# Moving GpSimd's arithmetic to VectorE and storing T by head in a chunked delta-rule attention with two expert layers

## Chip, cores and metric

One core of one Trainium2 chip runs the whole program. The metric is device time in microseconds (us) of one execution; lower is better. The kernel before takes 1076.54 us, the median of 3 runs (1076.4 to 1076.81).

## What is computed

Three layers follow each other. The first is the one that the change touches: for each of 4 batches and 8 heads a 48 x 48 state is carried over 768 tokens, and every token's key corrects it.

```python
state = zeros((B, H, D, D))                      # B, H, D = 4, 8, 48
for t in range(S):                               # S = 768, k_n = normalised k
    y[:, :, t] = einsum('bhd,bhde->bhe', q[:, :, t], state)
    v_old = einsum('bhde,bhd->bhe', state, kt)
    state = state + bt * einsum('bhd,bhe->bhde', kt, vt - v_old)
```

The 3072 result rows of 384 numbers then go through a top-1 layer of 8 experts (384 to 1024 to 384, with a gate) and a gated dense layer (384 to 1536 to 384).

## The kernel before

The sequence is cut into 24 chunks of 32 tokens (`CH`, `NSTEP`). One chunk is a **step** s; four steps are a **group** g, two steps a pair u. The four batches lie in the 128 partitions, 32 tokens each. Inside a chunk the recurrence is solved with a triangular matrix T of 32 x 32 for each head and batch, so that a step is a few matmuls, written out in order in the loop of `Attention.run` (line 751):

- **KS** (line 778): state times key, 16 matmuls with stationary operand `KB[...][:, p, :, h]`; VectorE makes `W` from it (line 780).
- **Y**, first half (line 795): state times query from `QB`, 16 matmuls.
- **U** (line 804): T times W, 16 matmuls. The stationary operand is taken out of `TBD` with a step of 32 elements between its 64 columns (line 805). ScalarE writes the fp16 high part `UH[:, 0]` (line 807), VectorE the low part (line 811).
- **XTP** (`gate_t`), the expert gate's transposes for the step before; **GP** (`gp_mm`), the key products of step s + 11, 12 of its 16 matmuls here and 4 at the end of the step; there is GP only for s below 13.
- **Sps** (line 844): the state's update from `KBD` and `UH`, in three passes of which only the third reads the low part; ScalarE copies the state to `SH`.
- **Y**, second half (line 850), from `PBD` and `UH`; **GL** (`gate_l`), six gate matmuls whose stationary operand `xt[:, c, r]` has its 64 columns side by side.

Each fp32 matmul stands in the trace as two records, so the blocks KS, Y and U have 32 each, GP 24 and 8, GL 12.

Every engine runs its instructions in the order of the program. What is put between the instructions above comes from hand-set places and from a planner, `Filler` (line 99): it holds the chain that makes the next group's T and the gate's small operations, with a planned duration for each, and `fil.run(budget)` issues as many as the budget covers. A step has a budget of `TA` = 2.4 us between the W and the low part of UH (line 806) and of `TB` = 4.2 us (`TC` = 3.8 us from step 12 on) at its end (line 906). At the end of a group, lines 910 to 912 issue whatever is left of the next group's T at one go.

The T of a group is made by `prep` (line 330: transposing, normalising, `scale`) and `inv_ops` (line 387: 31 columns j, each one product `tmp<-X,Lt` and one sum `X<-X,tmp` over min(j + 1, share) rows of 31 - j elements, in one or two parts). Rows from `SHE[g]` on (24 for group 2, 20 for groups 3 to 5; none for group 1) are GpSimd's. `last` (line 441) turns X into `XT`; `expand_t` (line 379) copies the 8 columns that the first step of the group needs into `TBD`, and later, in that step, the other 24: two quarters by VectorE (line 813), two by ScalarE (line 874).

GpSimd's other work in the steps: `scale` for groups 2 to 5 (line 341, all 32 rows), `v_mul` (202), `p_split` (276), `p_split_lo` (290), `kh_split_lo` (316), and `scatter` (574) with its indirect DMA. SyncE (SP) issues all other DMAs, among them `kexp` (322) and `expand` (293), each four DMAs that spread `KH` and `PHL` into `KBD` and `PBD`.

Of the kernel before, what the change touches and what calls it, by code (L numbers as in the profile page):

```python
# [7 lines left out]
F32 = mybir.dt.float32  # L8
# [5 lines left out]
ALU = mybir.AluOpType  # L14
# [20 lines left out]
LA = 11  # L35
# [9 lines left out]
XE = (0, 1, 2, 3, 4, 5)  # L45
# [4 lines left out]
WE = 1.0  # L50
TC = 3.8
NR = 8
Q2 = 0.0
GS = 6
KA = 1
SHE = (0, 32, 24, 20, 20, 20)
TA = 2.4
TB = 4.2
W0 = 36
# [39 lines left out]
class Filler:  # L99
# [41 lines left out]
class Attention:  # L141
# [5 lines left out]
    def run(self, small, acc, zero_fill, small_loads):  # L147
# [23 lines left out]
        QB = [cp.tile([128, 2, 64, 8], F32, name=f"QB{i}") for i in range(2)]  # L171
        TBD = [(cp if i else ep).tile([128, 2, 1024], F32, name=f"TBD{i}") for i in range(2)]
        PBD = [cp.tile([128, 2, 16, 4, 32], F16, name=f"PBD{i}") for i in range(2)]
# [18 lines left out]
        def load_kth(u):  # L192
            t = wk.tile([128, 2, 48, 8], F32, tag="kth", name="kth", bufs=1)
            SP.dma_start(out=t.rearrange("p s d h -> p s (d h)"), in_=a["ktok"][:, 2 * u : 2 * u + 2])
            KTOK[u] = t
# [5 lines left out]

        def v_mul(s):
            g, s4 = divmod(s, 4)
            v = VT[s // 2][:, s % 2].rearrange("p (h e) -> p h e", h=8)
            G.tensor_tensor(out=v, in0=v, in1=nt[:, g, 8 * s4 : 8 * s4 + 8].unsqueeze(2).to_broadcast([128, 8, 48]), op=ALU.mult)

# [68 lines left out]

        def p_split(u):
            g, i = divmod(u, 2)
            if g:
                pm = GPM[g][1][:, 16 * i : 16 * i + 16]
                G.tensor_tensor(out=pm, in0=pm, in1=rnt[:, g, 16 * i : 16 * i + 16].unsqueeze(2).to_broadcast([128, 16, 32]), op=ALU.mult)  # L280
            else:
                pm = PM.pop(u)
            G.tensor_tensor(out=pm, in0=pm, in1=mask.unsqueeze(1).to_broadcast([128, 16, 32]), op=ALU.mult)
            PHL[u] = wk.tile([128, 2, 16, 32], F16, tag="PHL", name="PHL", bufs=4)
            PMS[u] = pm
# [3 lines left out]

        def p_split_lo(u):  # L290
            G.tensor_tensor(out=PHL[u][:, 1], in0=PMS.pop(u), in1=PHL[u][:, 0], op=ALU.subtract)

# [23 lines left out]
        def kh_split_lo(u):  # L316
            KH, src = KHG[u], KTOK.pop(u)
            for s in range(2):
                G.tensor_tensor(out=KH[:, s, 1], in0=by_head(src[:, s]), in1=KH[:, s, 0], op=ALU.subtract)

# [9 lines left out]
        def prep(g):  # L330
# [9 lines left out]

            def scale(E, j0, j1, i0):
                L = Lt[:, j0:j1, i0:]
                E.tensor_tensor(out=L, in0=L, in1=x[:, j0:j1].unsqueeze(2).to_broadcast([128, j1 - j0, 32 - i0]), op=ALU.mult)
                E.tensor_tensor(out=L, in0=L, in1=nbr[:, g, i0:].unsqueeze(1).to_broadcast([128, j1 - j0, 32 - i0]), op=ALU.mult)


# [18 lines left out]
            ]  # L365
            sc = [(0.0, 0.0, lambda: scale(G, R, 32, R))]
            if R:
                sc.append((R / 12.0, 0.0, lambda: scale(V, 0, R, 0)))
            return ops, sc

        XTS, others = {}, []

        def share_rows(n):
# [5 lines left out]
        def expand_t(g, bs, ks):  # L379
            for E, b in zip((V, V, A, A), range(4)):  # L380
                if b in bs:
                    r = slice(32 * b, 32 * b + 32)
                    src = XTS[g][r].rearrange("p i b -> p (i b)").rearrange("p (i b) -> p i b", b=32)
                    dst = TBD[g % 2][r, b % 2].rearrange("p (i b) -> p i b", b=32)
                    (E.copy if E is A else E.tensor_copy)(out=dst[:, :, ks], in_=src[:, :, ks])

        def inv_ops(g, share=32):
# [53 lines left out]
            def last(F):  # L441
                share_rows(99)
                XT = wk.tile([128, 32, 32], F32, tag="XT", name="XT", bufs=1)
                V.transpose(out=XT.rearrange("p i b -> p (i b)"), in_=X.rearrange("p k i -> p i k"))
                F.t += 1.135
                F.ready = F.t
                F.done = g
                XTS[g] = XT
                if g == 0:
                    V.memset(zl, 0.0)  # L450
                if g in XE:
                    expand_t(g, range(4), slice(0, 8))
                else:
                    for b in range(4):
                        r = slice(32 * b, 32 * b + 32)
                        SP.dma_start(out=TBD[g % 2][r, b % 2], in_=XT[r].rearrange("p i b -> p (i b)"))

# [169 lines left out]
        SP.dma_start(out=be, in_=a["beta"])  # L627
        SHz = wk.tile([128, 2, 384], F32, tag="SH", name="SH", bufs=2)
        V.memset(SHz.rearrange("p b c -> p (b c)"), 0.0)
# [67 lines left out]
        p_split(0)  # L697
        zero_fill(SP, 0, TBD[1])
        p_evac(2)
# [5 lines left out]
        gp(9)  # L705
        zero_fill(SP, 1, TBD[1])
        load_kth(1)
# [27 lines left out]
        load_kth(2)  # L735
        zero_fill(SP, 2, TBD[1])
        busy(Sps[0], D.get(0, 0))
# [13 lines left out]
        for s in range(NSTEP):  # L751
# [12 lines left out]
            beside(s, "load", engines)  # L764
            if s2 == 0 and 0 < s < NSTEP - 2:
                kh_split_lo(u + 1)
            if s2 == 1 and u + 3 < NSTEP // 2:
                p_split(u + 3)
            if s > 0:
# [16 lines left out]
            if s2 == 0 and 0 < s < NSTEP - 2:  # L786
                expand(PBD[(u + 1) % 2], PHL.pop(u + 1))
                if half:
                    load_kth(u + 2)
                kexp(u + 1)  # L790

# [46 lines left out]
            if not last:  # L838
                SH = wk.tile([128, 2, 384], F32, tag="SH", name="SH", bufs=2)
# [676 lines left out]
```

## Time and profile before

| What | us |
|---|---|
| median of 3 runs | 1076.54 |
| the profiled execution | 1079.49 |
| its span, first to last instruction | 1077.8 |
| TensorE (PE) busy in it | 1022.6 |
| VectorE (DVE) busy | 569.2 |
| GpSimd (POOL) busy | 430.2 |
| ScalarE (ACT) busy | 416.9 |

The 24 steps lie between 65 and 348 us of the span; what is before prepares group 0, what is behind is the two expert layers, and the change leaves both as they are but for T's layout. Busy shares are averages; a wait counts only where it ends last. PEclk is the granted share of TensorE's 2.4 GHz: 1.00 is 2.4 GHz, 0.50 is 1.2 GHz, and a mean between them says how the stretch is divided between the two levels. Matmuls are pipelined: a record's duration says little, and the time from the start of one block to the start of the next is what the block costs.

### The profile page before, as it was taken

Reading aid. Unit: us, or ns where it says so; the run is one execution under the profiler, and the core shown is the slowest. Engines: PE = TensorE matmul, PEld = TensorE weight load, DVE = VectorE, ACT = ScalarE, POOL = GpSimd, SP = SyncE. Lnnn points to the kernel's source line nnn. Section 1 sums busy time; section 2 is a strip of 40 time slices with the busy share of each in tenths; the row PEclk is TensorE's granted clock in tenths of the full one; section 3 lists DMA queues with packets and bytes.
Section 4 is the critical chain, followed back from the end, with each engine's and each line's share of the span. In section 5 each row is a group of like instructions: output and inputs, shape, how many; then the busy total and the mean of one; then the engine's idle time right before and its main releaser. Section 6 shows DMA issues by size and latency. Waiting matters only on the chain. (4 is left out here: it accounts for less than half of the span.)

```text
span 1077.8 us, 22538 instructions
## 1 busy us (share of the span) xinstructions
PE 1022.6 (95%) x9111; PEld 926.5 (86%) x9112; DVE 569.2 (53%) x1376; ACT 416.9 (39%) x892; POOL 430.2 (40%) x460
## 2 busy tenths in 40 slices
PE   8788999997899999899899899999999999999997
PEld 8777989897898988789889888888888888888886
DVE  6978899989965587667673364511211211211211
ACT  6644646474563444454445232311212222212111
POOL 8455456665733235444444134322322311321322
PEclk8976865566569999999999999999999999999999
DMA  7899977644485365455643222000000000000000
GB/s 187 200 175 201 193 151 142 141 92 86 88 160 133 126 208 155 150 160 171 181 117 117 46 60 74 23 23 1 18 12 1 30 1 1 30 1 1 30 1 30
DMA packets 162622, 100.11 MB, mean 93 GB/s; under 512 B 108025, under 2 KB 152002, under 8 KB 162514
## 3 DMA queue, kind: packets, MB, share of 16 engines
q1 hardware_dynamic: 159442, 89.17, 35.8%
q0 software_dynamic: 3072, 9.46, 2.4%
q8 instruction: 73, 1.20, 0.5%
q14 instruction: 35, 0.29, 0.1%
HBM read 74.94 MB, written 15.80 MB: 84 GB/s over the span
## 5 line engine op out<-in xcount | busy, mean ns | idle before, releaser
L1437 DVE TENSOR_TENSOR gf<-gf,g 128x512 f32<-128x512 f32 x72 | 49.5, 688 | 312.0 <-PE g L1429 310.3
L938 POOL TENSOR_TENSOR gsl<-gf,gsh 128x512 fp32r<-128x512 f32 x68 | 88.7, 1305 | 272.1 <-ACT gsh L937 272.1
L1436 ACT ACTIVATE gf<-g 128x512 f32<-128x512 f32 x72 | 43.0, 597 | 190.8 <-PE g L1429 188.8
L937 ACT CAST gsh<-gf 128x512 fp32r<-128x512 f32 x69 | 42.8, 620 | 144.4 <-DVE gf L1437 142.5
L87 DVE TENSOR_TENSOR X<-X,tmp 128x60 f32<-128x60 f32 (+25 forms) x282 | 96.1, 367 | 1.2
L87 DVE TENSOR_TENSOR tmp<-X,Lt 128x60 f32<-128x60 f32 (+25 forms) x282 | 94.7, 362 | 1.9
L1403 PE MATMUL o<-woh,gsl 128*128 128x384 f32 x272 | 87.3, 339 | 0.0
L1403 PE MATMUL o<-wol,gsh 128*128 128x384 f32 x272 | 86.5, 337 | 0.0
L1118 DVE SCALAR_TENSOR_TENSOR hl<-h,hh 128x460 fp32r<-128x460 f32 (+7 forms) x57 | 33.1, 580 | 61.6 <-ACT hh L1117 61.4
L1429 PE MATMUL g<-yl,wgh 128*128 128x512 f32 x216 | 62.6, 395 | 0.0
L1429 PE MATMUL g<-yl,wvh 128*128 128x512 f32 x216 | 62.3, 395 | 0.0
L1077 PE MATMUL y<-hh,w2h 128*128 128x460 f32 (+6 forms) x168 | 60.8, 362 | 1.2 <-ACT hh L1117 1.0
L1403 PE MATMUL o<-woh,gsh 128*128 128x384 f32 x272 | 61.7, 337 | 0.0
L1429 PE MATMUL g<-yh,wgh 128*128 128x512 f32 x180 | 61.0, 395 | 0.0
L1077 PE MATMUL y<-hh,w2l 128*128 128x460 f32 (+6 forms) x168 | 58.6, 349 | 0.0
L87 ACT ACTIVATE kth<-kth,rnt 128x48 f32<-128x48 f32 x192 | 54.8, 375 | 6.9 <-DMA kth<-in_ktok_dram 6.6
L87 PE MATMUL GP<-KT,KB 112*64 112x64 f32 x640 | 47.8, 315 | 10.2 <-POOL KH L87 7.0
L87 PE MATMUL U<-W,TBD 64*64 64x48 f32 x768 | 47.9, 292 | 8.5 <-DVE W L87 8.5
L87 PEld LDWEIGHTS GP<-KT,KB 112*64 112x64 f32 x640 | 42.6, 221 | 14.7 <-POOL KH L87 7.1
L1403 PEld LDWEIGHTS o<-woh,gsh 128*128 128x128 f32 x272 | 49.7, 188 | 5.8
L87 PEld LDWEIGHTS U<-W,TBD 64*64 64x64 f32 x768 | 44.4, 200 | 10.6 <-DVE W L87 9.2
L1055 POOL TENSOR_TENSOR w1l<-w1r,w1h 128x768 fp32r<-128x768 f32 x19 | 37.2, 1957 | 39.9 <-ACT w1h L1050 39.6
(330 smaller groups left out, 2490.4 us busy)
## 6 DMA issues: line engine op xcount, KB each, us to landing
w1r<-in_w_dram SPq DMA_DIRECT2D x32, 384.0 KB
w2r<-in_w_dram SPq DMA_DIRECT2D x32, 384.0 KB
KT<-in_st_dram SPq DMA_DIRECT2D x20, 448.0 KB
disp<-TBD SPq DMA_DIRECT2D x8, 772.0 KB
kth<-in_ktok_dram SPq DMA_DIRECT2D x12, 384.0 KB
VT<-in_vtok_dram SPq DMA_DIRECT2D x12, 384.0 KB
KBD<-KH SPq DMA_DIRECT2D x48, 96.0 KB
XG<-in_m2g_dram SPq DMA_DIRECT2D x12, 384.0 KB
```

What stands on the lines that cost most here:

```text
L87: r = f(*args, **kw)
L937: (act or nc.scalar).copy(out=hi, in_=src)
L938: eng.tensor_tensor(out=lo, in0=src, in1=hi, op=ALU.subtract)
L1055: engine.tensor_tensor(out=l, in0=self.raw[b][i], in1=h, op=ALU.subtract)
L1077: self.T.matmul(out=ys[c][:, 0:n], lhsT=w2[l][:, f % 2, 128 * c : 128 * c + 128], rhs=(hh, hl)[r], start=(f == 0 and i == 0), stop=(f == 7 ...
L1118: self.V.scalar_tensor_tensor(out=hl, in0=hp[:, 0:n], scalar=0.0, in1=hh, op0=ALU.max, op1=ALU.subtract)
L1403: T.matmul(out=ops_[m][:, 0:384], lhsT=gh[l][:, 128 * m : 128 * m + 128], rhs=wo[r][:, f], start=(f == 0 and i == 0), stop=(f == 11 and i ...
L1429: T.matmul(out=ps, lhsT=gv[w][l][:, c, 128 * f : 128 * f + 128], rhs=Y[r][c], start=(i == 0 and c == 0), stop=(i == 2 and c == 2))
L1436: A.activation(out=gf, in_=gps[0], func=AF.Sigmoid)
L1437: V.tensor_tensor(out=gf, in0=gf, in1=gps[1], op=ALU.mult)
```

## The change

`TBD` holds T as [k, b, i], k being the head and step, so that the 64 columns (b, i) of one head lie side by side. The last 24 of its 32 k are now spread by four DMAs on SP's queue (`expand_rest`) instead of by VectorE and ScalarE. In the steps, `v_mul`, `p_split`, `p_split_lo`, `kh_split_lo`, and `scale` for groups 2 to 5 run on VectorE; `scale` then skips most of the half that is zero (six instructions over 256, 192 and 256 elements). No row of the inverse is left to GpSimd. Step 0 keeps `p_split(2)`, `v_mul(2)` and the first `p_split_lo` on GpSimd. `kh_split_lo` and `p_split` move from the head of the step to behind the low part of UH, `kexp` from behind W to the step's end. `kth` gets a second buffer and `SH` loses its own. The planner's budgets change, and `spend` takes the moved work off them.

```diff
-TC = 3.8
+TC = 4.4
-SHE = (0, 32, 24, 20, 20, 20)
+SHE = (0, 32, 32, 32, 32, 32)
-TB = 4.2
+TP = 2.5
+TB = 5.8
...
+    def spend(self, dur):
+        self.t = max(self.t, self.until) + dur
...
-        TBD = [(cp if i else ep).tile([128, 2, 1024], F32, name=f"TBD{i}") for i in range(2)]
+        TBD = [(cp if i else ep).tile([128, 32, 2, 32], F32, name=f"TBD{i}") for i in range(2)]
...
-        def v_mul(s):
+        def v_mul(s, E=G):
             g, s4 = divmod(s, 4)
+            norms(g)
...
-            sc = [(0.0, 0.0, lambda: scale(G, R, 32, R))]
             if R:
-                sc.append((R / 12.0, 0.0, lambda: scale(V, 0, R, 0)))
-            return ops, sc
+                sc = [(0.0, 0.0, lambda: scale(G, R, 32, R)), (R / 12.0, 0.0, lambda: scale(V, 0, R, 0))]
+            else:
+                sc = [(0.1 + (j1 - j0) * (32 - i0) / 1200.0, GAP, lambda f=f, r=(j0, j1, i0): f(V, *r))
+                      for f in (by_row, by_col) for j0, j1, i0 in ((0, 8, 0), (8, 16, 8), (16, 32, 16))]
+            return ops + [(0.0, 0.0, lambda: normed.add(g))], sc
...
+        def expand_rest(g):
+            for b in range(4):
+                r = slice(32 * b, 32 * b + 32)
+                SP.dma_start(out=TBD[g % 2][r, 8:32, b % 2], in_=XTS[g][r, 8:32])
...
-                V.transpose(out=XT.rearrange("p i b -> p (i b)"), in_=X.rearrange("p k i -> p i k"))
+                V.transpose(out=XT.rearrange("p b i -> p i b"), in_=X.rearrange("p k i -> p i k"))
...
-                mm(out=Up[r, h], lhsT=TBD[g % 2][r].rearrange("p b k -> p (b k)")[:, 8 * s4 + h :: 32], rhs=W[r, h], start=True, stop=True)
+                mm(out=Up[r, h], lhsT=TBD[g % 2][r, 8 * s4 + h].rearrange("p b i -> p (b i)"), rhs=W[r, h], start=True, stop=True)
...
             V.tensor_tensor(out=UH[:, 1], in0=Up, in1=UH[:, 0], op=ALU.subtract)
             if s4 == 0 and g in XE:
-                expand_t(g, (0, 1), slice(8, 32))
+                expand_rest(g)
+            if s2 == 0:
+                if 0 < s < NSTEP - 2:
+                    kh_split_lo(u + 1, V)
+                    fil.spend(0.95)
+            elif u + 3 < NSTEP // 2:
+                p_split(u + 3, V)
+                fil.spend(1.2)
...
             if s + 2 < NSTEP and s:
-                v_mul(s + 2)
+                v_mul(s + 2, V)
+                fil.spend(0.48)
...
             if s2 == 1 and u + 3 < NSTEP // 2:
                 p_split_hi(u + 3)
-                p_split_lo(u + 3)
+                fil.run(TP)
+                p_split_lo(u + 3, V)
+                fil.spend(0.6)
...
+            if s2 == 0 and 0 < s < NSTEP - 2:
+                kexp(u + 1)
             beside(s, "end", engines)
-            fil.run(((TB if s + 1 + LA < NSTEP else TC) - (0.94 if s4 == 0 and g in XE else 0.0)) if s else TB0)
+            fil.run(((TB - (TP if s2 == 1 and u + 3 < NSTEP // 2 else 0.0) if s + 1 + LA < NSTEP else TC)) if s else TB0)
```

## Rows read from the trace of the kernel before

**Rows 1.** Stretches: us, then busy us of each engine, PEclk, DMA share, GB/s.

```profile
65.00:348.00 283.00, 260.76 (x4729) 245.10 (x4728) 239.38 (x727) 153.01 (x379) 149.96 (x201) 0.67 0.72 142
165.47:178.02 12.55, 12.55 (x220) 11.79 (x219) 12.08 (x43) 8.30 (x20) 8.01 (x13) 0.50 0.96 156
218.38:229.36 10.98, 10.98 (x219) 10.45 (x218) 9.31 (x34) 7.91 (x20) 6.77 (x10) 0.78 0.47 83
315.30:346.00 30.70, 29.66 (x599) 27.72 (x597) 15.01 (x46) 15.36 (x33) 12.66 (x16) 1.00 0.65 140
320.08:329.02 8.94, 8.94 (x194) 8.47 (x190) 4.50 (x12) 5.86 (x12) 4.35 (x5) 1.00 0.79 162
```

**Rows 2.** Waits between 65 and 345 us: us in total, times, longest us.

```profile
POOL PHL L87 <- ACT PHL L87: 63.2, 11, 15.7
...
PE Sps L87 <- DVE UH L87: 12.9, 6, 5.3
...
PE U L87 <- DVE W L87: 8.5, 5, 2.7
```

**Rows 3.** DVE's groups of instructions, 65 to 345 us: busy us, mean ns, idle before.

```profile
L87 DVE TENSOR_TENSOR X<-X,tmp 128x90 f32<-128x90 f32 (+34 forms) x226 | 81.5, 385 | 1.0
L87 DVE TENSOR_TENSOR tmp<-X,Lt 128x90 f32<-128x90 f32 (+34 forms) x226 | 81.0, 384 | 1.6
...
L87 DVE STREAM_TRANSPOSE XT<-X 128x1024 f32<-128x1024 f32 x5 | 9.8, 1969 | 0.3
...
L87 DVE COPY TBD<-XT 32x768 f32<-32x768 f32 x12 | 8.1, 671 | 0.1
```

**Rows 4.** DVE's timeline, 198 to 221 us: start us, duration us, instruction.

```profile
198.25 0.34 DVE L87 TENSOR_TENSOR X<-X,tmp 128x240 f32<-128x240 f32 x1
198.51 1.89 DVE L87 SCALAR_TENSOR_TENSOR nbr<-bx,be 128x32 f32<-128x32 f32 x1
...
200.92 2.32 DVE L87 TENSOR_TENSOR X<-X,tmp 128x220 f32<-128x220 f32 x1
...
212.40 0.22 DVE L87 TENSOR_TENSOR tmp<-X,Lt 128x60 f32<-128x60 f32 x1
...
220.66 0.55 DVE L87 SCALAR_TENSOR_TENSOR W<-VT,KS 128x384 f32<-128x384 f32 x1
```

**Rows 5.** POOL's timeline at the same time.

```profile
198.41 1.95 POOL L87 TENSOR_TENSOR Lt<-Lt,bx 128x1024 f32<-128x1024 f32 x1 [0.17 <-DVE bx L87]
200.55 2.44 POOL L87 TENSOR_TENSOR Lt<-Lt,nbr 128x1024 f32<-128x1024 f32 x1 [0.19 <-DVE g_pos L87]
```

**Rows 6.** PE's timeline, blocks of step 9 (1.2 GHz) and step 12 (2.4 GHz).

```profile
181.97 2.02 PE L87 MATMUL U<-W,TBD 64*64 64x48 f32 x32
183.92 0.90 PE L87 MATMUL XTP<-cst,XG 128*128 128x128 f32 x3
...
189.41 0.83 PE L87 MATMUL GL<-wgo,xt 128*64 128x16 f32 x12
190.17 0.21 PE L87 MATMUL GL<-g_oh,lt 128*128 128x32 f16 x1
...
222.36 1.98 PE L87 MATMUL U<-W,TBD 64*64 64x48 f32 x32
224.26 0.55 PE L87 MATMUL XTP<-cst,XG 128*128 128x128 f32 x3
...
228.45 0.53 PE L87 MATMUL GL<-wgo,xt 128*64 128x16 f32 x12
228.82 0.73 PE L87 MATMUL GP<-KT,KB 112*64 112x64 f32 x8
```

**Rows 7.** SP's timeline in step 0: DMAs issued.

```profile
68.50 3.38 SPq L87 DMA_DIRECT2D KB<-in_st_dram  x2
71.98 5.34 SPq L87 DMA_DIRECT2D PBD<-PHL  x4
```

More of the change, by code (lines that the diff above doesn't have):

```diff
@@ L192, in load_kth @@
         def load_kth(u):
-            t = wk.tile([128, 2, 48, 8], F32, tag="kth", name="kth", bufs=1)
+            t = wk.tile([128, 2, 48, 8], F32, tag="kth", name="kth", bufs=2)
             SP.dma_start(out=t.rearrange("p s d h -> p s (d h)"), in_=a["ktok"][:, 2 * u : 2 * u + 2])
@@ L200, in load_v @@
             VT[u] = t
-        def v_mul(s):
+        def v_mul(s, E=G):
             g, s4 = divmod(s, 4)
+            norms(g)
             v = VT[s // 2][:, s % 2].rearrange("p (h e) -> p h e", h=8)
-            G.tensor_tensor(out=v, in0=v, in1=nt[:, g, 8 * s4 : 8 * s4 + 8].unsqueeze(2).to_broadcast([128, 8, 48]), op=ALU.mult)
+            E.tensor_tensor(out=v, in0=v, in1=nt[:, g, 8 * s4 : 8 * s4 + 8].unsqueeze(2).to_broadcast([128, 8, 48]), op=ALU.mult)
         GPS = {}
@@ L274, in run, with p_split @@
         PMS = {}
-        def p_split(u):
+        def p_split(u, E=G):
             g, i = divmod(u, 2)
             if g:
+                norms(g)
                 pm = GPM[g][1][:, 16 * i : 16 * i + 16]
-                G.tensor_tensor(out=pm, in0=pm, in1=rnt[:, g, 16 * i : 16 * i + 16].unsqueeze(2).to_broadcast([128, 16, 32]), op=ALU.mult)
+                E.tensor_tensor(out=pm, in0=pm, in1=rnt[:, g, 16 * i : 16 * i + 16].unsqueeze(2).to_broadcast([128, 16, 32]), op=ALU.mult)
             else:
                 pm = PM.pop(u)
-            G.tensor_tensor(out=pm, in0=pm, in1=mask.unsqueeze(1).to_broadcast([128, 16, 32]), op=ALU.mult)
+            E.tensor_tensor(out=pm, in0=pm, in1=mask.unsqueeze(1).to_broadcast([128, 16, 32]), op=ALU.mult)
             PHL[u] = wk.tile([128, 2, 16, 32], F16, tag="PHL", name="PHL", bufs=4)
@@ L288, in p_split_hi, with p_split_lo @@
             A.copy(out=PHL[u][:, 0], in_=PMS[u])
-        def p_split_lo(u):
-            G.tensor_tensor(out=PHL[u][:, 1], in0=PMS.pop(u), in1=PHL[u][:, 0], op=ALU.subtract)
+        def p_split_lo(u, E=G):
+            E.tensor_tensor(out=PHL[u][:, 1], in0=PMS.pop(u), in1=PHL[u][:, 0], op=ALU.subtract)
         def expand(dst, src):
@@ L298, in kh_mul @@
         def kh_mul(u, half=None):
+            norms(u // 2)
             r = rnt[:, u // 2].rearrange("p (s h) -> p s h", s=4)
@@ L314, in kh_split_hi, with kh_split_lo @@
             KHG[u] = KH
-        def kh_split_lo(u):
+        def kh_split_lo(u, E=G):
             KH, src = KHG[u], KTOK.pop(u)
             for s in range(2):
-                G.tensor_tensor(out=KH[:, s, 1], in0=by_head(src[:, s]), in1=KH[:, s, 0], op=ALU.subtract)
+                E.tensor_tensor(out=KH[:, s, 1], in0=by_head(src[:, s]), in1=KH[:, s, 0], op=ALU.subtract)
         def kexp(u):
@@ L339, in prep, with by_row, by_col, scale @@
             tr = lambda o, i, d: (d, 0.0, lambda: V.transpose(out=o, in_=i))
-            def scale(E, j0, j1, i0):
+            def by_row(E, j0, j1, i0):
                 L = Lt[:, j0:j1, i0:]
                 E.tensor_tensor(out=L, in0=L, in1=x[:, j0:j1].unsqueeze(2).to_broadcast([128, j1 - j0, 32 - i0]), op=ALU.mult)
+            def by_col(E, j0, j1, i0):
+                L = Lt[:, j0:j1, i0:]
                 E.tensor_tensor(out=L, in0=L, in1=nbr[:, g, i0:].unsqueeze(1).to_broadcast([128, j1 - j0, 32 - i0]), op=ALU.mult)
+            def scale(E, *r):
+                by_row(E, *r)
+                by_col(E, *r)
             ops = [
@@ L365, in prep, with norms @@
             ]
-            sc = [(0.0, 0.0, lambda: scale(G, R, 32, R))]
             if R:
-                sc.append((R / 12.0, 0.0, lambda: scale(V, 0, R, 0)))
-            return ops, sc
+                sc = [(0.0, 0.0, lambda: scale(G, R, 32, R)), (R / 12.0, 0.0, lambda: scale(V, 0, R, 0))]
[3 more added lines that the diff above has]
+            return ops + [(0.0, 0.0, lambda: normed.add(g))], sc
+        normed = set()
+        def norms(g):
+            while g not in normed:
+                fil.step()
         XTS, others = {}, []
+        zeros = TBD[1].rearrange("p k b i -> p (k b i)").rearrange("p (b x) -> p b x", b=2)
         def share_rows(n):
@@ L382, in expand_t @@
                     r = slice(32 * b, 32 * b + 32)
-                    src = XTS[g][r].rearrange("p i b -> p (i b)").rearrange("p (i b) -> p i b", b=32)
-                    dst = TBD[g % 2][r, b % 2].rearrange("p (i b) -> p i b", b=32)
-                    (E.copy if E is A else E.tensor_copy)(out=dst[:, :, ks], in_=src[:, :, ks])
+                    (E.copy if E is A else E.tensor_copy)(out=TBD[g % 2][r, ks, b % 2], in_=XTS[g][r, ks])
+        def expand_rest(g):
+            for b in range(4):
+                r = slice(32 * b, 32 * b + 32)
+                SP.dma_start(out=TBD[g % 2][r, 8:32, b % 2], in_=XTS[g][r, 8:32])
         def inv_ops(g, share=32):
@@ L455, in last @@
                         r = slice(32 * b, 32 * b + 32)
-                        SP.dma_start(out=TBD[g % 2][r, b % 2], in_=XT[r].rearrange("p i b -> p (i b)"))
+                        SP.dma_start(out=TBD[g % 2][r, :, b % 2], in_=XT[r])
             other = [(lambda j=j: add(G, j, share, j + 1, mul(G, j, share, j + 1))) for j in range(share, 31)]
@@ L627, in run @@
         SP.dma_start(out=be, in_=a["beta"])
-        SHz = wk.tile([128, 2, 384], F32, tag="SH", name="SH", bufs=2)
+        SHz = wk.tile([128, 2, 384], F32, tag="SH", name="SH", bufs=1)
         V.memset(SHz.rearrange("p b c -> p (b c)"), 0.0)
@@ L697, in run @@
         p_split(0)
-        zero_fill(SP, 0, TBD[1])
+        zero_fill(SP, 0, zeros)
         p_evac(2)
@@ L705, in run @@
         gp(9)
-        zero_fill(SP, 1, TBD[1])
+        zero_fill(SP, 1, zeros)
         load_kth(1)
@@ L735, in run @@
         load_kth(2)
-        zero_fill(SP, 2, TBD[1])
+        zero_fill(SP, 2, zeros)
         busy(Sps[0], D.get(0, 0))
@@ L764, in run @@
             beside(s, "load", engines)
[L765 to L768, printed above, removed]
             if s > 0:
@@ L789, in run @@
                     load_kth(u + 2)
-                kexp(u + 1)
             Yp = pp.tile([128, 8, 48], F32, tag="Y", name="Y")
@@ L838, in run @@
             if not last:
-                SH = wk.tile([128, 2, 384], F32, tag="SH", name="SH", bufs=2)
+                SH = wk.tile([128, 2, 384], F32, tag="SH", name="SH", bufs=1)
                 for p, i in ((0, 0), (0, 1), (0, 2), (1, 0), (1, 1), (1, 2)) if s < LS or not SP2 else ((0, 0), (0, 1), (1, 0), (1, 1), (0, 2), (1, 2)):
@@ L872, in run @@
                     v1 = fil.add(gate_v1(g - 1), WG)
-            if s4 == 0 and g in XE:
-                expand_t(g, (2, 3), slice(8, 32))
             if s2 == 1 and u + 3 < NSTEP // 2:
                 p_split_hi(u + 3)
-                p_split_lo(u + 3)
+                fil.run(TP)
+                p_split_lo(u + 3, V)
+                fil.spend(0.6)
             if more and s:
@@ L892, in run @@
             if s < 5:
-                zero_fill(SP, s + 3, TBD[1])
+                zero_fill(SP, s + 3, zeros)
             if s == 0:
```

## The prediction

> **What bounds the kernel now.** I read the stretches first. The steps take 283 of 1078 us, and only they are touched. In them PE is busy for 260.8 us, DVE for 239.4, POOL for 150.0, and the granted clock is 0.67 [rows 1]; as the levels are 0.5 and 1.0, 34% of the stage runs at 2.4 GHz. Step 8, in which PE never pauses, takes 12.55 us at 1.2 GHz; step 12, whose blocks behind U came after the clock had risen, takes 10.98 [rows 1]. So where nothing is late the step is PE's, and the low clock costs it 1.57 us. A step without GP at 2.4 GHz takes 8.94 us, and there the clock stayed up for 30.7 us on end [rows 1].
>
> The waits come second: PE stood 12.9 us for the low part of UH and 8.5 us for W, both DVE's: 21.4 us of stage that is neither PE's work nor its clock [rows 2].
>
> Why is DVE late? Its 452 products and sums of the inverse take 162.5 us [rows 3]. The same kind of instruction takes 0.22 us for 60 elements and 0.34 for 240, but one of 220 took 2.32, and a `nbr` of 32 elements 1.89 [rows 4]. These two lie on POOL's two passes of `scale`: `nbr` starts 0.10 us behind the first and ends with it, the 2.32 ends a quarter of a microsecond behind the second [rows 4, 5]. DVE stands while POOL reads.
>
> PE's blocks come last. U's 32 records take 1.95 us at 1.2 GHz and 1.90 at 2.4: 61 and 59 ns each. GL's, also with 64 fp32 columns, take 0.76 us for 12 at 1.2 GHz and 0.37 at 2.4: 63 and 31 ns [rows 6]. U's columns lie 128 bytes apart, GL's side by side; U gets nothing from the faster clock.
>
> **DVE's account.** Slope from 60 elements (0.22) to 240 (0.34) is 0.7 ns, but W's 384 at 0.55 and 60 at 0.22 give 1.0 ns; I take 1.0 and a base of 0.16 us, 0.08 of which overlaps the next instruction (the 0.34 is followed after 0.26) [rows 4]. Added, in occupied time:
> - `v_mul`, 21 of 384 elements at 0.47: 9.9 us.
> - `kh_split_lo`, 10 pairs of 384: 9.4 us. Its source is strided; the only long strided reads on DVE are the transposes of XT, 1.97 us for 1024 [rows 3], by which 384 take 0.74, so 5.4 us more is the upper end. I take the lower, from W, the nearest in kind.
> - `p_split`, 9 pairs of 512 at 0.59, and 9 `p_split_lo`: 16 us.
> - `scale`, four groups of six instructions, 1408 elements: 4 x (1.41 + 0.48) = 7.6 us.
> - GpSimd's rows of the inverse: 84 elements in group 2 and 286 in each of groups 3 to 5, twice over: 1.9 us.
>
> That is 45 us. The twelve `TBD` copies go, at about 0.5 each (8.1 us with what they lost to POOL [rows 3]): 6 us. Net +39. Against it the inverse: five times 5456 elements less GpSimd's 942, for product and sum, are 52.7 thousand elements, 53 us, and 452 x 0.08 = 36 us of base: 89 us where the trace has 162.5 [rows 3]. So 73 us were stood out, and 239.4 becomes about 239 - 73 + 39 = 205 us. XT's transpose now also writes with a stride; its read has one already, so I take 1.97 again, at most twice that, 10 us over five.
>
> **The terms, on the profiled 1079.49 us.**
> 1. PE's waits, 21.4 us. What stays late is the end of a group. The inverse of a group needs by the planner's own durations about 26 us (18 for the columns, 4.7 for `prep` with `scale`, 1.1 for XT, 2 for the gate). From step 12 on four steps give 4 x (2.4 + 4.4) less 7.4 of `spend`, 19.8 us. Some is worked ahead in steps 4 to 11 (32.8 - 7.4 = 25.4 a group, after a start with a lead of some 4); I expect 4 us flushed at step 15 and 2 at step 19, with W queued behind on DVE and PE waiting for W. 21.4 - 6: **-15.4**; bounds 0 and -21.4.
> 2. U. At 2.4 GHz a block goes from 1.90 us to 32 x 31 ns = 0.99: -0.91. At 1.2 GHz, 61 against 63 ns: nothing. With 60% of 24 steps at 2.4 GHz: 24 x 0.6 x 0.91 = **-13.1**; bounds 0 (layout without effect) and -21.8 (all steps at 2.4 GHz).
> 3. The clock. Nothing in the trace shows the clock of such a kernel; the nearest rows are the step without GP and without waits, which kept it, and the steps with GP, which did not though PE never paused [rows 1]. Eleven steps have no GP; I give them 0.9 and the thirteen others the old 0.34: 0.60. 24 x 0.26 x 1.57 = **-9.8**; bounds +12.8 (the share falls to nothing) and -24.9 (it is 1).
> 4. T by DMA. Four DMAs of 768 pieces each join SP's queue in the first step of each group. `PBD`'s four of 1024 pieces took 5.34 us to issue [rows 7]; three quarters are 4.0. SP has a whole step to issue and land them and U of the next step waits for them. In step 0 they queue behind `KB`, until 71.9 us, so the last is issued near 76 [rows 7], while U of step 1 could start, W no longer late, at about 76: I take **+1.5** once, between 0 and 4. They delay what is behind them on SP, `PBD` and the next loads, each needed a step later.
>
> Edits that I cost at nothing: ScalarE loses its copies and is busy for 153 of 283 us [rows 1]; `kexp` goes later, past `expand_rest` and `load_v` on SP, and may wait there for `kh_split_lo`, but `KBD` is needed in the middle of the next-but-one half step, some 10 us on (if that cover went, Sps would wait for 5 us of issue); one `SH` is enough, since KS and Y have read it, in PE's order, before Sps ends; `kth`'s second buffer only loosens.
>
> Sum: -15.4 - 13.1 - 9.8 + 1.5 = -36.8, so 1042.7 for the profiled execution; the median is 3.0 below that execution, so **1040** for the runs.
>
> **A rule that says otherwise.** At 2.4 GHz the 64 columns of GL cost 31 ns and those of U 59 [rows 6]. The Trainium skill, "TensorE: Matmul & The Clock Gate", section "LDWEIGHTS (loading the stationary operand)", says that the load takes the number of columns over 1.2 GHz and names nothing else; for 64 that is an estimate of 53 ns whatever the layout, and term 2 would be nothing. The trace disagrees at 2.4 GHz, where GL is below it, and agrees at 1.2.
>
> **The rivals.**
> - **Layout without effect.** U stays at 59 ns because its 64 x 64 tiles or its 48 moving columns set the pace, not the gaps (GL has 128 rows and 16 moving columns). Term 2 falls: 1053. For it: U differs from GL in all of these. Against: at 1.2 GHz the two cost the same [rows 6], so rows and moving columns don't part them there; the layout is left as the reason that only GL gains from the clock. 8%.
> - **The clock doesn't follow.** Steps 8 to 12 sat at 1.2 GHz with PE unbroken, so waits alone don't hold it down. Share 0.34: terms 2 and 3 are -7.4 and 0: 1079.5 - 15.4 - 7.4 + 1.5 - 3 = 1055. 20%.
> - **DVE becomes the bound.** 205 us in the 20 steps before the last inverse is done are over 10 us each, as much as a step with GP at 2.4 GHz and more than one without. If the bursts keep PE's waits at half, the strided split costs its 5 us and the clock follows the waits: 1079.5 - 8 - 7.4 + 1.5 - 3 = 1063. 12%.
> - **Slower: DVE takes over POOL's wait.** `p_split_lo` needs ScalarE's cast of `PHL`, which needs Y of the same step. POOL stood for that cast for 63.2 us in 11 waits, 5.7 us each [rows 2], with nothing urgent behind it. On DVE the filler and W stand behind it. PE has 1.3 us of cover (Y's 1.9 us less W's 0.55), so nine odd steps lose 9 x (5.7 - 1.3) = 40 us against the 36.8 gained: 1080. It decides from 36.8 / 9 + 1.3 = 5.4 us of standing. Against: `p_split`, `v_mul` and `fil.run(TP)`, 2.5 us by the plan, go first, and POOL's waits count from when it ran out of work. 8%.
>
> **How the numbers follow.** The forecast, all four terms in their middle, has 52%; it spans 1022 (all waits gone and 80% of the stage at 2.4 GHz: terms of -21.4, -17.5 and -17.3, with 1.5 back) to 1053. The range must reach over the two cases at 1053 and 1055 and nearly all of that at 1063: 1022 to 1063. Two thousandths, 2.2 us, is about what a measurement of this kernel tells from no change. Faster has the forecast and all faster rivals, 0.90 with part of the slower mechanism in a mild form; slower 0.08; within it 0.02.
>
> **What would show it.** In the changed profile: no POOL arithmetic between 75 and 345 us but the scatter's small copies, and DVE busy near 205; `nbr` at 0.2 us; PE's waits for UH and W near 6 us together, at the ends of groups 3 and 4; U's block at 1.0 us wherever PEclk is 1.00 and 1.9 elsewhere; PEclk near 0.8 in the steps. I am wrong if U's block is 1.9 us at PEclk 1.00, if DVE waits for ACT's `PHL` by more than 2 us a time, or if PE waits for a DMA into `TBD`.

## The result, and the profile after

The changed kernel takes 1091.59 us (median of 10 runs, 1086.08 to 1096.96), the kernel before 1077.51 on the same chip (10 runs, 1073.93 to 1085.01). The ratio is 1.0121 [1.0093, 1.015]: slower by 1.2%, where I had predicted 1040 us.

I cut both executions from the start of the first U to the end of the last `UH`, so that the steps stand by themselves. First the stretches of the kernel before: all steps, the last four (from U of step 20 to the end of U of step 23), the rest (columns as in [rows 1]).

```profile
65.75:345.71 279.96, 257.72 (x4673) 242.38 (x4671) 237.49 (x714) 152.15 (x375) 149.96 (x201) 0.67 0.73 143
314.65:344.59 29.94, 28.90 (x593) 27.26 (x592) 14.16 (x44) 14.80 (x31) 12.66 (x16) 0.99 0.70 150
345.71:1077.80 732.09, 710.96 (x3697) 633.16 (x3694) 278.53 (x489) 225.85 (x408) 236.59 (x178) 0.99 0.21 65
```

The same three of the changed kernel:

```profile
64.39:357.36 292.97, 256.00 (x4669) 239.45 (x4667) 215.23 (x766) 141.47 (x362) 32.97 (x45) 0.62 0.74 145
322.68:356.24 33.56, 33.56 (x591) 31.09 (x592) 15.00 (x46) 10.54 (x22) 5.76 (x8) 0.50 0.50 120
357.36:1090.00 732.64, 711.18 (x3700) 633.42 (x3698) 279.09 (x489) 226.31 (x408) 236.01 (x178) 0.99 0.21 65
```

The 13.0 us are all in the steps; the layers behind them keep their time. Span less busy time gives PE's idle time: 22.2 us before, 37.0 after, +14.8. PE's busy time falls by only 1.7. DVE did become lighter, 237.5 to 215.2, and then stood more: 42.5 us before, 77.7 after. So an engine with more room is waited for longer. In the last four steps PE never stands in the changed kernel, and they take 33.6 us at 1.2 GHz where they took 29.9 at 2.4.

The waits of the changed kernel between 65 and 358 us (answering to [rows 2]):

```profile
DVE UH L88 <- ACT UH L88: 38.1, 19, 5.5
...
PE U L88 <- DVE W L88: 24.0, 8, 7.6
...
DVE W L88 <- PE KS L88: 16.0, 8, 4.1
DVE PHL L88 <- ACT PHL L88: 15.2, 9, 3.0
...
PE U L88 <- DMA TBD<-XT: 5.6, 4, 3.5
...
PE Y L88 <- DMA QB<-in_st_dram: 5.0, 2, 3.0
...
PE Sps L88 <- DVE UH L88: 0.6, 1, 0.6
```

The wait for UH's low part, 12.9 us before [rows 2], is gone, as meant. The wait for W has grown from 8.5 to 24.0, and two waits for DMAs are new. Where W is late is seen in DVE's timeline at the end of a group (step 15 into 16; one line near 199 us first):

```profile
199.53 0.18 DVE L88 SCALAR_TENSOR_TENSOR nbr<-bx,be 128x32 f32<-128x32 f32 x1
...
264.32 0.69 DVE L88 TENSOR_TENSOR PHL<-P,PHL 128x512 f16<-128x512 f32 x1 [0.96 <-ACT PHL L88]
264.93 0.40 DVE L88 TENSOR_TENSOR X<-X,tmp 128x240 f32<-128x240 f32 x1
265.37 0.47 DVE L88 TENSOR_TENSOR tmp<-X,Lt 128x110 f32<-128x110 f32 x2
...
269.00 0.39 DVE L88 TENSOR_TENSOR tmp<-X,Lt 128x78 f32<-128x78 f32 x2
...
272.12 0.21 DVE L88 TENSOR_TENSOR X<-X,tmp 128x31 f32<-128x31 f32 x1
272.36 1.94 DVE L88 STREAM_TRANSPOSE XT<-X 128x1024 f32<-128x1024 f32 x1
274.34 0.58 DVE L88 COPY TBD<-XT 32x256 f32<-32x256 f32 x2
274.95 0.56 DVE L88 SCALAR_TENSOR_TENSOR W<-VT,KS 128x384 f32<-128x384 f32 x1
```

and in PE's timeline at that place and at the end of step 19, with one of U's blocks at 2.4 GHz and the one behind the first DMAs into `TBD` ahead of them:

```profile
77.09 0.41 PE L88 MATMUL U<-W,TBD 64*64 64x48 f32 x2 [3.46 <-DMA TBD<-XT]
78.88 1.41 PE L88 MATMUL U<-W,TBD 64*64 64x48 f32 x22 [1.37 <-DMA TBD<-XT]
...
91.39 1.15 PE L88 MATMUL U<-W,TBD 64*64 64x48 f32 x32
92.47 0.55 PE L88 MATMUL XTP<-cst,XG 128*128 128x128 f32 x3
...
263.85 2.15 PE L88 MATMUL KS<-SH,KB 128*64 128x48 f32 x32
...
275.56 1.95 PE L88 MATMUL U<-W,TBD 64*64 64x48 f32 x32 [7.63 <-DVE W L88]
277.44 0.90 PE L88 MATMUL XTP<-cst,XG 128*128 128x128 f32 x3
...
322.68 1.95 PE L88 MATMUL U<-W,TBD 64*64 64x48 f32 x32 [5.93 <-DVE W L88]
```

KS ended at 266.00, so W could have gone then. It goes at 274.95: the last eleven columns of the inverse (from 265.37 to 272.33), the transposition of XT and two copies stand in front of it on DVE, back to back. Columns 20 to 24 were issued by the last budget of step 15 itself; from column 25 on (269.00) it is what is left of the next group's T, issued at one go at the group's end. By the planner's own durations this remainder is 0, 1.9, 2.6, 4.3 and 3.2 us at the ends of steps 3, 7, 11, 15 and 19. Measured in the same way, from KS's end to W's start, W is late by 4.2, 4.9, 5.8, 9.0 and 6.5 us in steps 4, 8, 12, 16 and 20, and by 2.4 at most elsewhere; in the kernel before it is late by 1.1 at most in these five. In all five the transposition and the copies, about 2.6 us, run in front of W. In step 4 W is late although nothing was left over: what delays it is all that the planner places at the group's end, by budget or as a remainder.

DVE's groups (answering to [rows 3]):

```profile
L88 DVE TENSOR_TENSOR X<-X,tmp 128x60 f32<-128x60 f32 (+30 forms) x212 | 57.7, 295 | 0.9
L88 DVE TENSOR_TENSOR tmp<-X,Lt 128x60 f32<-128x60 f32 (+30 forms) x212 | 55.9, 287 | 1.3
L88 DVE TENSOR_TENSOR KH<-kth,KH 128x384 f16<-128x384 f32 x20 | 16.1, 842 | 0.0
...
L88 DVE TENSOR_TENSOR VT<-VT,nt 128x384 f32<-128x384 f32 x21 | 11.5, 548 | 0.0
L88 DVE STREAM_TRANSPOSE XT<-X 128x1024 f32<-128x1024 f32 x5 | 9.8, 1962 | 0.2
...
L88 DVE TENSOR_TENSOR P<-P,mask 128x512 f32<-128x512 f32 x9 | 7.1, 786 | 0.3
L88 DVE TENSOR_TENSOR PHL<-P,PHL 128x512 f16<-128x512 f32 x9 | 6.2, 692 | 15.2 <-ACT PHL L88 15.2
```

Although DVE now does GpSimd's rows too, its products and sums take 113.6 us where they took 162.5 [rows 3], and `nbr`, 1.89 us behind GpSimd's `scale` [rows 4], takes 0.18. The stalls by GpSimd are gone, as predicted.

SP's queue in step 0 (answering to [rows 7]): the issue of the DMAs into `TBD` ends at 76.1, the U that needs them starts at 77.09. The last two lines come later: the load of `QB` for step 6 stands behind `kexp`'s four DMAs, and Y of step 6 waits for `QB` until 142.47.

```profile
67.62 3.33 SPq L88 DMA_DIRECT2D KB<-in_st_dram  x2
71.05 5.05 SPq L88 DMA_DIRECT2D TBD<-XT  x4
76.20 2.82 SPq L88 DMA_DIRECT2D PBD<-PHL  x4
...
128.62 7.25 SPq L88 DMA_DIRECT2D KBD<-KH  x4
...
136.61 0.96 SPq L88 DMA_DIRECT2D QB<-in_st_dram  x2
```

### The profile page after: what moved, and what is told of

The parts are those of the page before. It is cut to its first block, busy times and chain, and to the rows that moved or that the text cites. A ratio compares the mean times of both kernels' runs of the same rounds, so it can differ in the third digit from the quotient of the medians.

```text
span 1090.0 us, 22431 instructions
## 1 busy us (share of the span) xinstructions
PE 1020.1 (94%) x9111; PEld 922.9 (85%) x9112; DVE 546.5 (50%) x1428; ACT 406.7 (37%) x880; POOL 312.5 (29%) x304
## 5 line engine op out<-in xcount | busy, mean ns | idle before, releaser
L88 DVE TENSOR_TENSOR X<-X,tmp 128x84 f32<-128x84 f32 (+33 forms) x268 | 73.5, 298 | 1.1
L88 PE MATMUL U<-W,TBD 64*64 64x48 f32 x768 | 43.1, 286 | 29.7 <-DVE W L88 24.0
L88 DVE TENSOR_TENSOR tmp<-X,Lt 128x84 f32<-128x84 f32 (+33 forms) x268 | 69.7, 285 | 1.6
L88 PEld LDWEIGHTS U<-W,TBD 64*64 64x64 f32 x768 | 39.3, 202 | 32.6 <-DVE W L88 25.4
L88 POOL COPY XG<-g_sc 128x2 f32<-128x2 f32 x24 | 7.5, 312 | 201.8 <-DVE g_sc L88 160.5
L88 PE MATMUL Y<-SH,QB 128*64 128x48 f32 x736 | 50.3, 313 | 5.0 <-DMA QB<-in_st_dram 5.0
```

What stands on the lines that cost most here:

```text
L88: r = f(*args, **kw)
```

## The experiments

The theory of the budgets: not DVE's speed holds up W, but what the planner doesn't place early in the steps and so leaves for the group's end, in front of it. Its rivals: the DMAs into `TBD`; the moved work itself, DVE being too full or waiting for ScalarE; the clock, which stays low by itself. All runs in one table; the columns of the steps are from the profiled execution, the ratio is to the kernel before, run on the same chip beside it. The rows e1 to e4 share a chip, so do f1 to f4 and g0 to g3; the kernel before took 1083.8, 1082.8 and 1084.0 us there, and the changed kernel was not run again beside them. f1 and g0 are one kernel, and their ratios differ by 0.45 points, so a difference of that size between rows of different chips shows nothing. A profiled execution is not the median either: e1's is the fastest of its seven, 6.7 us under it.

| Kernel | Steps, us | PE idle | PEclk | Last four steps (PEclk) | Ratio [interval] |
|---|---|---|---|---|---|
| before | 280.0 | 22.2 | 0.67 | 29.9 (0.99) | 1 |
| after | 293.0 | 37.0 | 0.62 | 33.6 (0.50) | 1.0121 [1.0093, 1.015] |
| e1_budget | 276.2 | 27.0 | 0.67 | 28.7 (0.96) | 0.9943 [0.9916, 0.9971] |
| e2_layout | 279.4 | 28.8 | 0.65 | 27.8 (0.94) | 0.9965 [0.994, 0.9989] |
| e3_copies | 290.0 | 32.5 | 0.61 | 33.5 (0.50) | 1.006 [1.0035, 1.0086] |
| e4_move | 294.2 | 28.8 | 0.57 | 33.8 (0.50) | 1.0092 [1.0061, 1.0123] |
| f1_budget_copies | 268.4 | 29.1 | 0.74 | 25.4 (1.00) | 0.9847 [0.9785, 0.9908] |
| f2_fill | 269.7 | 20.1 | 0.78 | 26.9 (1.00) | 0.984 [0.9773, 0.9907] |
| f3_tc6 | 271.0 | 25.3 | 0.69 | 25.7 (0.99) | 0.9898 [0.9846, 0.995] |
| f4_tc_alone | 289.4 | 37.7 | 0.64 | 26.2 (1.00) | 1.0006 [0.9975, 1.0037] |
| g0_again | 269.1 | 22.6 | 0.68 | 27.1 (0.98) | 0.9892 [0.9846, 0.9938] |
| g1_kh_back | 279.4 | 24.0 | 0.62 | 30.4 (0.84) | 0.9908 [0.9874, 0.9942] |
| g2_budget_old | 302.6 | 43.8 | 0.58 | 32.4 (0.61) | 1.0115 [1.0074, 1.0156] |
| g3_tp | 272.8 | 14.4 | 0.58 | 27.3 (0.97) | 0.9859 [0.9822, 0.9896] |

**e1_budget**: the changed kernel with larger budgets and nothing else.

```diff
-TC = 4.4
+TC = 5.4
-TA = 2.4
+TA = 3.4
```

> The changed kernel with larger planner budgets: TA 2.4 to 3.4 us, TC 4.4 to 5.4 us, nothing else. Theory P (the planner issues too little in the steps, so five group ends hold W up by 4.2 to 9.0 us behind KS while DVE stands idle for 79 us of the steps elsewhere): the 24 us that PE waits for W fall below 8, and the time to 1070 to 1078. Theory D (DVE has no time left, wherever the work is put): W is late in other steps instead, PE's wait for DVE stays at 20 us or more, and the time within 4 us of 1091.

Measured: 0.9943, faster than before and 1.8 points under the changed kernel. By the planner's durations nothing is left over at any group's end, and W is late by 2.1 us at most in steps 4, 8 and 12. 5.2, 4.3 and 3.6 remain in steps 14, 16, 17: the chains of groups 4 and 5 now end in the budgets at the ends of steps 13 and 16, still in front of W. So the wait for W falls to 11.0 us, not below 8:

```profile
PE U L88 <- DVE W L88: 11.0, 6, 3.9
...
PE U L88 <- DMA TBD<-XT: 6.5, 4, 4.1
```

The same arithmetic on the same engine, placed earlier, turns the loss into a gain. That speaks for the budgets, and the same two numbers changed on top of e3 (f1 and g0, below) bring 1.7 to 2.1 points; the loss doesn't lie in DVE's having the work.

**e2_layout**: the kernel before, with T by head alone (`XT`'s transpose and the engines' copies follow the layout).

```diff
-lhsT=TBD[g % 2][r].rearrange("p b k -> p (b k)")[:, 8 * s4 + h :: 32]
+lhsT=TBD[g % 2][r, 8 * s4 + h].rearrange("p b i -> p (b i)")
```

> The kernel before with T kept by head alone: GpSimd's arithmetic, planner and copies by VectorE and ScalarE stay. If the layout does what the trace of the change shows (29.6 against 55 ns a record at 2.4 GHz, 53 against 55 at 1.2), 24 blocks of which a third run at 2.4 GHz give 7 to 9 us: 1067 to 1071. If U's shorter block only makes PE wait longer for DVE, the time stays within 3 us of before.

Measured: 0.9965, 3.8 us, between the two expectations. Ten of U's 24 blocks ran at 2.4 GHz, at 29.6 ns from record to record where both clocks had given 55 before (my 61 and 59 counted in the passage to the next block); at 1.2 GHz 53. The layout works, but ten blocks by about 0.8 us are 8 us, and PE's idle time rose by 6.6: most of it went into waits for the same instructions of DVE (for UH 16.1 us, [rows 2] has 12.9).

**e3_copies**: the changed kernel, with T's last 24 columns copied by VectorE and ScalarE at the old places; **e4_move**: that with the old layout too, so the move and the planner's new numbers alone.

```diff
             if s4 == 0 and g in XE:
-                expand_rest(g)
+                expand_t(g, (0, 1), slice(8, 32))
...
+            if s4 == 0 and g in XE:
+                expand_t(g, (2, 3), slice(8, 32))
             if s2 == 1 and u + 3 < NSTEP // 2:
                 p_split_hi(u + 3)
```

> The changed kernel with the last 24 columns of T copied by VectorE and ScalarE at the places that they had before, instead of by four DMAs. If the DMAs cost what the waits show (TBD 5.6 us, QB 5.0 us behind them on the queue), PE waits for no TBD and the time falls by 5 to 10 us, to 1082 to 1087. If DVE is the bound, its 6 us of copies put W later and the time is 1091 or more.

> GpSimd's work moved to VectorE and the changed planner, but T in the old layout and spread by the engines' copies. Theory P: the group ends still hold W up by about 25 us in all; against the run with copies and the new layout it lacks U's gain, 4 to 8 us: 1088 to 1096, so slower than before by 1 to 2%. If the layout or its DMAs were what made the change slow, this run is at or below the time before, 1077.

Measured: 1.006 and 1.0092. The DMAs seem to cost about 0.6% (1.0121 to 1.006, on two chips): they are a part of the loss, the smaller one. In the profiles the steps are 3.0 us shorter and PE's wait for `TBD` is gone, but the one for `QB` stays:

```profile
PE Y L88 <- DMA QB<-in_st_dram: 4.1, 2, 3.6
```

The layout gives about 0.3%, as in e2, though the two intervals overlap. The move with the change's budgets is by itself slower than the kernel before, and W's row stands as in the changed kernel (e3):

```profile
PE U L88 <- DVE W L88: 26.0, 8, 7.7
```

**f1_budget_copies**: e3 with e1's budgets. **g0_again**: the same kernel on another chip.

> The larger budgets (TA 3.4, TC 5.4) together with T's last 24 columns copied by VectorE and ScalarE. If the two effects seen alone (-1.8% and -0.6% against the changed kernel) are independent, 0.986 to 0.992 of the kernel before. If DVE becomes the bound with the copies, PE's wait for W comes back to 20 us and the ratio is 0.994 or more.

> The budget-and-copies kernel once more, beside the three that differ from it or from the layout kernel by one thing: 0.982 to 0.991 of the kernel before.

Measured: 0.9847 and 0.9892, faster than before by 1.5 and 1.1%; within the intervals the two parts add up. W is still waited for by 16.3 and 13.8 us. Its eight runs go from 1063.5 to 1076.1 us with a mean granted clock of the whole program between 0.92 and 0.88.

**f4_tc_alone**: the changed kernel with `TC` 6.4 and no other edit; it is in use from step 12 on, so only the last two groups can change.

```diff
-TC = 4.4
+TC = 6.4
```

> The changed kernel with TC 4.4 to 6.4 us alone, which touches only steps 12 and later. Theory P, in its place: W's lateness at steps 16 and 20 (9.0 and 6.5 us) falls below 3 us each while that at steps 4, 8 and 12 (4.2, 4.9, 5.8) stays; 0.3 to 1.0% faster than the changed kernel, 1.002 to 1.009 of the kernel before. If lateness at the group ends has another cause, it stays in all five places.

Measured: 1.0006. In steps 4, 8 and 12 W is as late as in the changed kernel (4.2, 5.0, 5.8), and in step 20 by nothing, as the theory has it. But in step 16 it is late by 6.7, where I had less than 3, though the planner leaves nothing over in step 15; and in steps 14 and 18 it is now late by 4.9 and 4.2 (2.4 and 1.8 in the changed kernel). A larger budget at the step's end empties the remainder and itself stands in front of W. PE waits for W by 20.5 us in place of 24.0, and its idle time is no smaller. What is gained is clock, in the last four steps:

```profile
326.28:352.45 26.17, 25.79 (x593) 24.18 (x592) 15.01 (x46) 10.32 (x22) 4.85 (x8) 1.00 0.80 168
```

The same work takes 26.2 us at 2.4 GHz and 33.6 at 1.2 in the changed kernel, both with PE all but unbroken. (Of the 8.1 us between the two profiles 3.6 lie in all steps together; 4.3 lie in the layers behind, which the edit doesn't touch.) All three kernels in which PE stood 5.9 to 6.0 us for W of step 20 (after, e3, e4) run these steps at 0.50; of the others, none of which stood there, nine are at 0.94 or more, g1 at 0.84 and g2 at 0.61. So the stand in front of step 20 goes with a low clock behind it: 5.9 us of waiting and up to 7.4 of clock. That the one brings the other is not shown. In the changed kernel the clock was at 1.2 GHz from 303.1 to 316.7 us already, rose to 2.4 as PE stood, and had fallen again at 320.1, before PE went on at 322.68. Why the clock doesn't come back in 33.6 us of unbroken work is not shown.

**f3_tc6**: f1 with its budgets placed otherwise.

```diff
-TC = 5.4
+TC = 6.0
-TA = 3.4
+TA = 3.0
```

> As the budget-and-copies run, with TA 3.0 and TC 6.0. Theory P: what counts is that the sum over a group covers the inverse, so the time is within 5 us of that run. If the place of the work counts more than the sum (work between W and UH's low part is free, work at the step's end delays W), this is 5 us or more slower.

Measured: 0.9898, within f1's and g0's intervals, but by the medians on the same chip 7.0 us slower than f1 (1072.98 against 1065.95), on the side of the second expectation. f1's four runs lie up to 8.3 us apart, so neither is decided. With f4's steps 14, 16 and 18 it speaks for the place: budget at the step's end stands in front of W.

**g2_budget_old**: e2, so with GpSimd's arithmetic where it was, and `TA` 3.4.

```diff
-TA = 2.4
+TA = 3.4
```

> The layout kernel (GpSimd keeps its work, T by head) with TA 2.4 to 3.4 us. If the larger budget alone is what made the changed kernel fast, this gains as much, 8 to 15 us against the layout kernel's 0.9965 of before. If it pays only because VectorE no longer stands for GpSimd, it gains nothing here or loses: VectorE, held up, reaches UH's low part later and PE's wait for it grows from 16 us.

Measured: 1.0115, slower by 1.5 points than e2 (on another chip). Its waits:

```profile
PE Sps L87 <- DVE UH L87: 24.5, 11, 5.3
...
PE U L87 <- DVE W L87: 16.9, 6, 4.1
```

The budget alone is no improvement: what is planned between W and UH's low part must fit there, and while GpSimd holds DVE up (its products and sums take 363 ns each here and 279 in e1) it doesn't. g2 raises `TA` alone, e1 `TC` too. So, as I read it, the move makes room, and the budget spends it; the change as it stood did the first and hardly the second.

**g1_kh_back**: f1 with `kh_split_lo` on GpSimd again.

```diff
-                    kh_split_lo(u + 1, V)
+                    kh_split_lo(u + 1)
```

> The budget-and-copies kernel with kh_split_lo back on GpSimd, all else and the planner's account unchanged. VectorE took 842 ns for each of the 20 strided subtractions, 16 us in all; GpSimd took 1171. If GpSimd's reading holds VectorE up for as long as it lasts, VectorE stands for about 20 us and nothing is gained: within 4 us of the kernel with it on VectorE, or slower. If the holding up is a small part, VectorE is 10 us or more lighter and the time falls by 3 to 8 us.

Measured: 0.9908, beside g0's 0.9892 on the same chip, with overlapping intervals: taking 16 us off DVE gains nothing. On GpSimd the instruction takes longer, and it isn't free for DVE:

```profile
L88 POOL TENSOR_TENSOR KH<-kth,KH 128x384 f16<-128x384 f32 x20 | 25.0, 1270 | 145.8 <-ACT KH L88 79.8 <-DMA QB<-in_st_dram 27.6 <-DMA VT<-in_vtok_dram 21.5
```

DVE's busy time in the steps is 221.9 us in g1, 223.1 in f1 and 222.7 in g0: without 16.1 us of its own instructions DVE is as long busy, the rest having stretched by as much. Most of that is in the products and sums of the inverse, 128.1 us where g0 has 116.2.

**f2_fill**: f1 with eight matmuls of zeros ahead of every U, against the clock theory; **g3_tp**: f1 with 4.0 us in place of 2.5 of filler ahead of `p_split_lo`, against the wait for ScalarE.

```diff
-            if s == 0:
-                for _ in range(B0):
-                    mm(out=Uf[:, 384:512], lhsT=zl, rhs=zl, start=True, stop=True)
+            for _ in range(B0):
+                mm(out=Uf[:, 384:512], lhsT=zl, rhs=zl, start=True, stop=True)
```

```diff
-TP = 2.5
+TP = 4.0
```

> The run before this one plus 8 matmuls of zeros (128 x 128 fp16, 56 ns each at 2.4 GHz, 107 at 1.2) between Y and U of every step, so that PE idles less and the strided stretch from KS to U is broken up; the output is the same. If low work of PE in this stretch is what keeps its clock at 1.2 GHz, the share of the steps at 2.4 GHz rises from a third to over two thirds and the time falls by 5 to 15 us against the run without. If the clock doesn't follow, 24 steps pay 0.4 to 0.9 us each: 10 to 20 us slower.

> The budget-and-copies kernel with TP 2.5 to 4.0 us: more filler ahead of p_split_lo, as much less behind it. VectorE's standing for ScalarE's cast of PHL, 9.5 us in 7 waits, falls below 4 us. If that standing delays W, the time falls by 2 to 5 us; if it lies in time that VectorE would have stood for UH or KS anyway, it is unchanged within 2 us.

Measured: 0.984 and 0.9859. Stretches of all steps, of f1, f2 and g3:

```profile
62.38:330.82 268.44, 239.39 (x4673) 224.97 (x4671) 223.15 (x814) 152.08 (x375) 31.61 (x45) 0.74 0.75 149
```

```profile
63.55:333.25 269.70, 249.62 (x4857) 232.67 (x4855) 223.46 (x814) 151.50 (x375) 32.01 (x45) 0.78 0.74 149
```

```profile
64.49:337.26 272.77, 258.42 (x4673) 241.93 (x4671) 224.60 (x816) 152.05 (x375) 32.99 (x45) 0.58 0.72 147
```

The zeros raise the share at 2.4 GHz from 48 to 56%, and PE is busy for 10.2 us longer all the same: no net gain. That the zeros raise the clock holds in all four runs of f2: the mean of the whole program is 0.921 to 0.954 there and 0.88 to 0.92 in the eight of f1 and g0. In g3 DVE's wait for ScalarE's `PHL` is down from 10.0 us in g0 to this:

```profile
DVE PHL L88 <- ACT PHL L88: 0.9, 1, 0.9
```

W is late by 0.3 us at most in steps 4, 8 and 12 (2.0 in g0), PE's idle time is the least of all, 14.4 us, and the clock nearly the lowest, 0.58; the time is that of f1 and g0 within the intervals. So the wait for `PHL` is real, but taking it out brings no time here, and fewer pauses of PE don't of themselves make the clock rise. What sets the clock stays open.

## Why the prediction was wrong

**Term 1 failed, and with it the sign.** I wrote that "I expect 4 us flushed at step 15 and 2 at step 19", 21.4 us of waits becoming 6. Half of it held: UH's wait fell from 12.9 to 0.6, and DVE's stalls by GpSimd went. But W is late at all five group ends, not two, by 4.2 to 9.0 us; 24.0 us of waits for W came where I had 6, so that the waits for DVE grew by 3.2. The step that failed is that I took PE's wait for what is flushed. The remainders of steps 15 and 19 were nearly as I had them, 4.3 and 3.2 by the planner's durations, and those of steps 7 and 11, where I had "a lead of some 4", 1.9 and 2.6. (My 19.8 us for steps 12 to 15 left out the `TP` of steps 13 and 15, which `TC` does not cover: it is 24.8.) But what the step's own budget issues at its end runs in front of W as well, and DVE is behind the plan by then: the planner counts 1.1 us for XT's transposition, nothing for the copies and 0.95 for a pair of `kh_split_lo`, which took 1.96, 0.6 and 1.68; with the smaller ones an estimate of 4 us a group. So a group's end is paid in one piece, in front of the one instruction on which PE waits, while DVE stands elsewhere (77.7 us). e1 and f1 show that budgets earlier in the step take most of it away; how much is remainder and how much DVE's lag is not shown apart.

**Term 3 had the wrong sign.** I had the share at 2.4 GHz go from 0.34 to 0.60; PEclk 0.62 makes it 0.24. The rival in which the clock doesn't follow, 20%, came true and more. One place is seen: the last four steps, 33.6 us against 29.9 before, though PE stood 1.0 us before and not at all after. (Steps 8 to 12 of the kernel before were not wholly unbroken, as I had it: PE stood 2.2 us for W in step 11.)

**Term 2 was right in size by block and wrong in count.** From U's start to the next block's it is 1.08 us (91.39 to 92.47) where I had 0.99, and 1.88 at 1.2 GHz (275.56 to 277.44). (The block of step 12 that I read as one at 2.4 GHz, [rows 6], began 0.7 us before the clock rose; that it cost the same was right, since blocks wholly at 2.4 GHz have the same 55 ns.) But only 5 of 24 blocks ran at 2.4 GHz where I had 60%: -4 us in place of -13.1. The rival of a layout without effect is refuted, by e2 too. The Trainium skill, "TensorE: Matmul & The Clock Gate", section "LDWEIGHTS (loading the stationary operand)", would have it at an estimate of 53 ns for any layout; the trace agrees at 1.2 GHz (53.0) and not at 2.4 (29.6).

**Term 4 was too small.** I took +1.5 once. PE stood 5.6 us for `TBD`, 4.8 of them in step 1: over my bound of 4. It stood a new 5.0 us for `QB`, which I had at nothing, taking what is behind on SP to be "needed a step later". The DMAs into `TBD` do not explain that one, since e3, without them, has 4.1 of it. The load of `QB` stands behind `kexp`'s DMAs, which wait for `kh_split_lo` (22.7 us in seven waits) and take 7.3 us to issue where they took 3.8 before (from 97.73 to 101.55 us there); I had costed `kexp`'s move at nothing by `KBD`'s own need alone. No run moves `kexp` back by itself, so this is argued. e3 puts the DMAs into `TBD` at 3.0 us of the steps, and at about 0.6%, some 6.5 us, by ratios from two chips.

**DVE's account.** I had 205 us; it is 215. `kh_split_lo` is 842 ns, not 470: I took the lower end, from W, and its strided source cost more than the upper end of 740. `p_split` takes 0.68 and 0.79 where I had 0.59. (The 113.6 us of the inverse are durations, whose overlaps count twice; my 91 left the overlaps out, 424 x 0.08 = 34 us, so that it came out some 11 us lighter than I had it.) None of this made DVE the bound: it stands for a quarter of the steps, so that rival fell.

**The slower rival** named DVE's taking over GpSimd's wait for `PHL`, deciding from 5.4 us a time. The wait is there, 15.2 us in 9, 1.7 each, and without it (g3, beside g0) the kernel is no faster. The kernel was slower for another reason than I had allowed for.

**How 13 us come about:** PE's waits +14.8 and its busy time -1.7, in which about 4 us saved in U are mostly given back by the lower clock. In my terms and at my prices: the waits for DVE +3.2 (I had -15.4), U -4 (-13.1), the clock 24 x 0.10 x 1.57 = +3.8 (-9.8), the waits for DMAs +10.6 (+1.5), together +13.6. With `TC` raised alone (f4) the kernel is level with before, with `TA` and `TC` raised (e1) it gains 0.6%, without the DMAs as well (f1) 1.1 to 1.5%.

## What to carry to other kernels

When work is moved off an engine that held another up, the static plan must be made again: budgets that were as large as the hindered engine could bear leave the new room unused, and the end of the chain lands in one piece in front of the instruction that everything waits for. So look first at what a planner puts there, left over or within its budget, and sum it with measured durations, the chain's last long step among them; a few microseconds there are a wait of as many. Judge an operation moved to save another engine by the busy time of both: g1 shows work given away that came back as stretched instructions.

## What the runs showed of the hardware that I had not expected

- The granted clock of these steps isn't set by PE's pauses alone: 0.58 with 14.4 us idle (g3), 0.74 with 29.1 (f1), and 0.50 through 33.56 us without any pause (the changed kernel's last four steps).
- One kernel's granted clock differs between runs on one chip: f1 had 0.92, 0.917, 0.897 and 0.88 with 1063.96, 1063.45, 1067.93 and 1071.76 us.
- On VectorE 384 fp32 elements took 842 ns where the source is read with a step of 8 elements (`KH<-kth,KH`) and 548 where it is contiguous (`VT<-VT,nt`; 556 with a result in fp16, as the strided one has, `UH<-U,UH`); on GpSimd the strided form took 1270.
